# Float16 from the fourth set on: its preparation moved ahead, and its loads begun on ScalarE

## The chip, the cores and the metric

One core of a Trainium2 chip runs the whole program. The metric is the device time of one execution in microseconds; the kernel before took 2170.98 us, the median of three runs.

The engines have short names in the profile: PE (TensorE, the matmuls), PEld (its weight loads), DVE (VectorE), ACT (ScalarE), POOL (GpSimd) and SP (SyncE, which here only starts transfers). Each works through its own list of instructions in order.

## What is computed

A Fourier filter along the sequence, and then a sparse mixture of eight two-layer experts on its result, two of them per row:

```
y = irfft(rfft(x, axis=1) * (filt_r + 1j * filt_i))        # x: 8 x 2496 x 256
x = y.reshape(19968, 256)
noisy = x @ w_gate + log1p(exp(x @ w_noise)) * noise       # 8 experts
top2, top2_w = the two largest, and their softmax
for e in range(8):
    for k in range(2):
        mask = top2[:, k] == e
        h = maximum(x[mask] @ w1[e], 0)                    # 256 -> 1024
        out[mask] += top2_w[mask, k, None] * (h @ w2[e])   # 1024 -> 256
```

## The kernel before

**Sets and blocks.** The 8 batches are Fourier-transformed one after the other. After each one, `gate` and `route` choose experts and append the rows to lists of the experts in HBM. Whenever a batch is done, some blocks of 512 rows of one expert are certain to be full, and the program runs them while it transforms the next batch. I call the blocks that become possible with batch n set n. Blocks are numbered from 0: set 1 is blocks 0 and 1, set 2 is 2 to 11, set 3 is 12 to 17, set 4 is 18 to 23 (three pairs that share an expert's weights), set 5 is 24 to 33, and so on. At the end come shorter blocks.

**One block** (`expert`). POOL gathers 4 x 128 rows of y; they are transposed and split in two parts, xT. Layer 1 makes eight tiles `hps` of 128 x 512 in PSUM. Each product of two split numbers is three matmuls (`_mm3`, lines 124 to 126): high x high, high x low, low x high. For each tile ACT writes the high part of the relu, `hh` (L1371), and DVE the rest, the residual `hl` (L1372). Layer 2 makes four tiles `yps` of 128 x 256, which ACT scales by the gate (L1399) and POOL adds to the output in HBM (L1400). So a block has 48 matmuls in layer 1 and 96 in layer 2.

**Two forms of a split.** Up to set HALF - 1 = 4, high and low parts are fp32r, four bytes each. From set HALF = 5 on they are float16, which needs scales (powers of two) so that nothing leaves its range: one scale for y up to each batch (`xscale`), and two for each expert's weights (`wtab`).

**The scales of the weights** come from `wscales`, a generator of 88 or so steps that also loads, splits and stores all weights for the short blocks at the end. Its first part, up to the scales, must be done when the first float16 block is gathered. `run` takes one step of it for every READY / NPREP yields of `expert` (13 yields a block), with READY = 13 * 24 - 32 = 280 before. The steps are:

- 64 loads of a quarter of an expert's w1 or w2 into one of two buffers `wp` (`load`, L598, issued on SP), and two steps behind each the sum of its squares on ACT (`top`, L603). After every fourth, DVE takes the maximum over the four quarter sums (L605).
- two transforms of maxima into powers of two (`powers`, L555 to L577): a transpose on PE, about ten small operations on DVE, two matmuls `xm` on PE that spread the result over all partitions, and a copy to `wtab` (L648 to L652).
- 12 loads of y of the first two batches (L615, on SP, into the same buffers) and their maxima on DVE (`top_y`, L620). Later batches are reduced while y is still on the chip (L546).

POOL copies the scales of a slot's expert out of `wtab` (L1149), and with them the weights are split (L1203, L1204).

**What sets the order.** The program is written as one stream. A scheduler then places each instruction by its own model of time, within the dependencies. `pin` adds order among some instructions of an engine, and `self.after(i)` places an instruction behind i. The Fourier steps fill gaps between expert matmuls, so that PE's list mixes both.

## Time and profile before

| | us |
|---|---|
| median of three runs (2166.45, 2170.98, 2173.87) | 2170.98 |
| the profiled execution | 2166.25 |
| its span, first to last instruction | 2164.4 |
| PE busy in the span | 2096.1 (97%) |
| PEld | 1595.0 (74%) |
| DVE | 1468.0 (68%) |
| ACT | 1286.9 (59%) |
| POOL | 1023.6 (47%) |

Busy time is the union of an engine's instructions; PE's overlap, so a busy PE is not PE at its peak. What a change is worth is read from the stage that it touches, and there from the wait that ends last.

### The profile page before, as it was taken

What the parts mean: (1) busy time and instruction counts of PE and PEld (TensorE: products, weight loads), DVE (VectorE), ACT (ScalarE), POOL (GpSimd) and SP (SyncE); (2) the same over time, 40 slices, a digit from 0 to 9 for tenths busy, and PEclk for the clock granted to TensorE, in tenths of its full rate; (3) what the DMA queues carried; (4) which work ended last, traced back from release to release, by engine and by line L of the source; (5) the groups of instructions that cost most, each with busy time, mean ns of one, the idle gap of its engine ahead of it and who ended that gap; (6) DMA issues with size and microseconds to landing.
All of it is one profiled execution on the core that took longest, in us unless ns stands there. A gap on an engine that the chain in (4) does not pass through costs nothing.

```text
span 2164.4 us, 42794 instructions
## 1 busy us (share of the span) xinstructions
PE 2096.1 (97%) x14517; PEld 1595.0 (74%) x14517; DVE 1468.0 (68%) x3221; ACT 1286.9 (59%) x2505; POOL 1023.6 (47%) x946
## 2 busy tenths in 40 slices
PE   8779999999999999999999999999999999999997
PEld 6447888888888888666766677666666666667886
DVE  4866779787977896688665976589666664433443
ACT  6666875787676455756664565555566564333443
POOL 4223434443443334445444453555655565654554
PEclk9989999999999999999999999999999999999999
DMA  9688989998999766767766787666889999779997
GB/s 255 181 253 223 234 211 225 239 243 219 231 218 219 158 149 143 178 143 188 155 151 130 151 182 165 145 123 132 235 207 240 239 250 235 166 145 228 268 276 189
DMA packets 511673, 428.48 MB, mean 198 GB/s; under 512 B 215679, under 2 KB 397015, under 8 KB 511447
## 3 DMA queue, kind: packets, MB, share of 16 engines
q1 hardware_dynamic: 450135, 341.27, 59.2%
q0 software_dynamic: 61312, 84.40, 23.0%
q8 instruction: 116, 1.90, 0.4%
q14 instruction: 110, 0.90, 0.1%
HBM read 263.92 MB, written 122.03 MB: 178 GB/s over the span
## 4 chain that ended last, share of the span: by engine, by line
PE 84%; DVE 4%; DMA 3%; issue 3%; ACT 3%; SPq 1%; POOL 1%; POOLq 0%; ACTq 0%; DVEq 0%
PE yps L126 12%; PE yps L124 12%; PE yps L125 12%; PE hps L124 12%; PE hps L125 11%; PE hps L126 11%; PE q L448 3%; PE q L509 1%; PE u L461 1%; PE q L337 1%; DMA wp<-y 1%; ACT yt L541 1%; DVE hl L1372 1%; PE q L533 1%; DMA stage<-w 1%
## 5 line engine op out<-in xcount | busy, mean ns | idle before, releaser
L1372 DVE SCALAR_TENSOR_TENSOR hl<-hps,hh 128x512 f16<-128x512 f32 (+3 forms) x712 | 432.8, 624 | 357.4 <-ACT hh L1371 276.7
L1400 POOL DMA_INDIRECT out<-stage,ids x316 | 530.6, 1679 | 264.4 <-ACT stage L1399 171.9
L1158 POOL DMA_INDIRECT stage<-y,ids x316 | 348.7, 1103 | 541.8 <-DMA xt<-stage 441.0
L124 PE MATMUL yps<-w,hh 128*128 128x256 f16 (+1 forms) x2048 | 556.7, 278 | 5.1 <-ACT hh L1371 2.4
L125 PE MATMUL yps<-w,hh 128*128 128x256 f16 (+1 forms) x2048 | 551.2, 277 | 0.0
L126 PE MATMUL yps<-w,hl 128*128 128x256 f16 (+1 forms) x2048 | 541.5, 277 | 1.9 <-DVE hl L1372 1.8
L1371 ACT ACTIVATE hh<-hps 128x512 f16<-128x512 f32 (+3 forms) x712 | 376.2, 550 | 197.0 <-PE hps L126 172.9
L125 PE MATMUL hps<-mxl,w1h 128*128 128x512 f16 (+1 forms) x1024 | 394.3, 386 | 2.2 <-DVE mxl L1246 1.3
L126 PE MATMUL hps<-mxh,w1l 128*128 128x512 f16 (+1 forms) x1024 | 393.9, 385 | 0.0
L124 PE MATMUL hps<-mxh,w1h 128*128 128x512 f16 (+1 forms) x1024 | 385.7, 388 | 7.5 <-DVE hl L1372 6.7
L1399 ACT ACTIVATE stage<-yps,gt 128x256 f32<-128x256 f32 x316 | 143.2, 476 | 346.8 <-PE yps L126 192.0
L124 PEld LDWEIGHTS <-hh 128*128 128x128 f16 x1760 | 172.2, 98 | 54.4 <-issue 6.4
L126 PEld LDWEIGHTS <-hl 128*128 128x128 f16 x1760 | 171.4, 98 | 48.6 <-DVE hl L1372 2.4
L125 PEld LDWEIGHTS <-hh 128*128 128x128 f16 x1760 | 172.3, 98 | 34.3 <-issue 2.6
L124 PEld LDWEIGHTS yps<-w,hh 128*128 128x128 f32 x768 | 145.6, 190 | 11.4 <-ACT hh L1371 1.6
L126 PEld LDWEIGHTS yps<-w,hl 128*128 128x128 f32 x768 | 144.7, 190 | 10.5 <-DVE hl L1372 2.0
L125 PEld LDWEIGHTS yps<-w,hh 128*128 128x128 f32 x768 | 145.0, 190 | 4.5
L126 PEld LDWEIGHTS <-w1l 128*128 128x128 f16 x640 | 62.6, 98 | 71.7 <-issue 1.5
L541 ACT COPY yt<-q 117x1024 uint16<-117x1024 uint16 x96 | 90.7, 945 | 39.0 <-PE q L535 29.1
L1228 DVE COPY stage<-xt 128x1024 uint16<-128x1024 uint16 (+2 forms) x174 | 110.6, 689 | 1.4 <-issue 1.4
L1108 POOL CAST ids<-lt 128x4 int32<-128x4 f32 (+3 forms) x66 | 22.3, 338 | 171.8 <-DMA lt<-lst 171.6
L125 PEld LDWEIGHTS <-w1h 128*128 128x128 f16 x640 | 62.6, 98 | 52.9 <-issue 4.8
(286 smaller groups left out, 4067.0 us busy)
## 6 DMA issues: line engine op xcount, KB each, us to landing
stage<-w SPq DMA_DIRECT2D x328, 256.0 KB
x<-x SPq DMA_DIRECT2D x88, 256.0 KB
fd<-c SPq DMA_DIRECT2D x77, 240.0 KB
fi<-wpl SPq DMA_DIRECT2D x18, 1024.0 KB
fx<-fd SPq DMA_DIRECT2D x140, 128.0 KB
out<-z SPq DMA_DIRECT2D x24, 702.0 KB
wp<-w SPq DMA_DIRECT2D x64, 256.0 KB
fr<-w SPq DMA_DIRECT2D x16, 1024.0 KB
```

Of the source, the lines that this page charges most:

```text
L124: nc.tensor.matmul(o, lh, rh, start=start, stop=False)
L125: nc.tensor.matmul(o, lh, rl, start=False, stop=False)
L126: nc.tensor.matmul(o, ll, rh, start=False, stop=stop)
L448: nc.tensor.matmul(q3[:, :, 2 * j:2 * j + 2].rearrange("p b r -> p r b"), a[:, j], self.cV, start=True, stop=True)
L541: e = nc.scalar.copy(yt.bitcast(U16)[:, :k, :256].rearrange("p g (two d) -> p g two d", two=2), p.bitcast(U16)[:RP, :2 * m].rearrange("p ( ...
L1108: nc.gpsimd.tensor_copy(ids, t)
L1158: self.pin(lambda: nc.gpsimd.indirect_dma_start(out=x.bitcast(I32), out_offset=None, in_=self.y[:BLK + ready * ROWS], in_offset=bass.Indir ...
L1228: nc.vector.tensor_copy(xu.rearrange("p (t two) -> p two t", two=2), ent[3][0][:, 2 * kc:2 * kc + 2, :w])
L1371: self.relu = hold(lambda: nc.scalar.activation(h, p, AF.Relu))
L1372: v = hold(lambda: nc.vector.scalar_tensor_tensor(l, p, 0.0, hf[0], op0=ALU.max, op1=ALU.subtract))
L1399: nc.scalar.activation(o, p, AF.Copy, scale=gate[:, t])
L1400: a = nc.gpsimd.indirect_dma_start(out=self.io["out"][:BLK + ready * ROWS], out_offset=bass.IndirectOffsetOnAxis(ap=ids[:, t:t + 1], axis= ...
```

## The change

HALF goes from 5 to 4, so that set 4 (blocks 18 to 23) is computed in float16. READY becomes 13 * 18 - 62 = 172, so that the steps of the preparation come 1.95 yields apart instead of 3.2. The loads of weights for the sums of squares are issued by ACT instead of SP, behind the latest relu instead of behind SP's latest weight load. The loads and maxima of y move between the first 32 and the last 32 of these loads, ahead of the transforms. Their maxima on DVE, and those over the quarter sums, are placed behind the latest residual (`self.resid`); the latter also come two steps later and from two alternating buffers.

```diff
-HALF = 5
+HALF = 4
-READY = 13 * SETS[HALF - 2] - 32
+READY = 13 * SETS[HALF - 2] - 62
...
+        self.xst = cp.tile([128, NB, 2], F32, name="xst")
-        self.wquart = cp.tile([128, 4], F32, name="wquart")
+        self.wquart = cp.tile([128, 2, 4], F32, name="wquart")
...
-        t = self.xs[bt + 1] = self.cp.tile([128, 2], F32, name=f"xs{bt}")
+        t = self.xs[bt + 1] = self.xst[:, bt]
...
             t = self.P.tile([128, 512], F32, name="wp", bufs=2)
-            with self.after(self.spw):
-                nc.sync.dma_start(t, io["w1" if i < 4 * E else "w2"][i // 4 % E, i % 4])
+            with self.after(self.relu):
+                nc.scalar.dma_start(t, io["w1" if i < 4 * E else "w2"][i // 4 % E, i % 4])
             return t
 
         def top(i, t):
+            if i % 4 == 1 and i > 4:
+                quarts(i // 4 - 1)
             with self.after(self.relu):
-                nc.scalar.activation(t, t, AF.Square, accum_out=self.wquart[:, i % 4:i % 4 + 1])
-            if i % 4 == 3:
-                v.tensor_reduce(self.wmax[:, i // 4:i // 4 + 1], self.wquart, axis=AX.X, op=ALU.max)
+                nc.scalar.activation(t, t, AF.Square, accum_out=self.wquart[:, i // 4 % 2, i % 4:i % 4 + 1])
+
+        def quarts(a):
+            with self.after(self.resid):
+                v.tensor_reduce(self.wmax[:, a:a + 1], self.wquart[:, a % 2], axis=AX.X, op=ALU.max)
...
-            v.tensor_reduce(self.ymax[:RP, 2 * bt + h, g // 8:g // 8 + 1], t, axis=AX.X, op=ALU.max, apply_absolute_value=True)
+            with self.after(self.resid):
+                v.tensor_reduce(self.ymax[:RP, 2 * bt + h, g // 8:g // 8 + 1], t, axis=AX.X, op=ALU.max, apply_absolute_value=True)
...
-        yield from pairs(load, top, 8 * E)
+        yield from pairs(load, top, 0, 32)
+        yield from pairs(load_y, top_y, 0, len(Y))
+        self.known = True
+        while self.owed:
+            yield from self.xscale(self.owed.pop(0))
+        yield from pairs(load, top, 32, 8 * E)
+        quarts(2 * E - 1)
         for a, t in enumerate((TW1, TW2)):
...
-        yield from pairs(load_y, top_y, len(Y))
-        self.known = True
-        while self.owed:
-            yield from self.xscale(self.owed.pop(0))
...
+                self.resid = v
```

The scheduler moves more than the diff tells. The line numbers of the changed kernel are 1 to 9 higher from there on (L1371 becomes L1379, L1372 becomes L1380).

PE, before, at the end of block 16: its last second-layer matmuls (`yps`), three Fourier matmuls, and first-layer matmuls (`hps`) of block 17, of which 18 stand further ahead already.

```order
L125 MATMUL yps<-w_9333,hh 128x256
L126 MATMUL yps<-w_9333,hl 128x256
L345 MATMUL q_7661<-xh,hl 120x512
L346 MATMUL q_7661<-xh,hl 120x512
L347 MATMUL q_7661<-xl,hl 120x512
L124 MATMUL hps<-mxh_9468,w1h 128x512
L125 MATMUL hps<-mxl_9469,w1h 128x512
L126 MATMUL hps<-mxh_9468,w1l 128x512
```

PE, changed, at the end of block 17: its last second-layer matmul, then the first weight transform (L559 to L576) among Fourier steps.

```order
L126 MATMUL yps<-w_9805,hl 128x256
L559 MATMUL xm<-ident,wmax 8x128
L510 MATMUL q_7732<-ident,G 120x128 x4
L576 MATMUL xm<-pd,small 128x8
L449 MATMUL q_7757<-cf,a 128x2x64 x4
L346 MATMUL q_7780<-xh,hl 120x512
L347 MATMUL q_7780<-xh,hl 120x512
L348 MATMUL q_7780<-xl,hl 120x512
L576 MATMUL xm<-pd,small 128x8
L559 MATMUL xm<-ident,wmax 8x128
```

Eight rows further on, the list ends with the second transform's last matmul and the first float16 matmul of block 18.

```order
L576 MATMUL xm<-pd,small 128x8
L449 MATMUL q_8048<-cf,a 128x2x64 x4
L346 MATMUL q_8074<-xh,hl 120x512
L347 MATMUL q_8074<-xh,hl 120x512
L348 MATMUL q_8074<-xl,hl 120x512
L124 LDWEIGHTS w1h
L124 MATMUL hps<-mxh_9915,w1h 128x512
```

Before, the two transforms stood in blocks 21 to 23, and matmuls of a block's second layer and of the next block's first mixed; now no expert matmul stands between the end of block 17 and the second transform's end.

DVE, before, at the end of block 17: maxima over re-read y (L620) ahead of and between residuals (L1372).

```order
L620 TENSOR_REDUCE ymax<-wp 117x1
L546 TENSOR_REDUCE ymax<-yt 117x1
L620 TENSOR_REDUCE ymax<-wp 117x1
L442 MEMSET G 128x80
L620 TENSOR_REDUCE ymax<-wp 117x1 x3
L1372 SCALAR_TENSOR_TENSOR hl<-hps,hh 128x512
L620 TENSOR_REDUCE ymax<-wp 117x1
L1372 SCALAR_TENSOR_TENSOR hl<-hps,hh 128x512
```

DVE, changed, in block 6: the same maxima (L626 now), each behind a residual (L1380 now), beside the gating of the third batch.

```order
L1380 SCALAR_TENSOR_TENSOR hl<-hps,hh 128x512
L626 TENSOR_REDUCE ymax<-wp 117x1
L961 TENSOR_REDUCE df<-rank_102 117x22
L943 CAST hb<-bi 128x8
L974 TENSOR_SCALAR row<-to,small 56x1
L1000 TENSOR_SCALAR ci<-ci 8x1
L1380 SCALAR_TENSOR_TENSOR hl<-hps,hh 128x512 x2
L626 TENSOR_REDUCE ymax<-wp 117x1
```

All twelve moved from blocks 16 to 20 into blocks 5 to 7.

ACT, changed, from the last relu (L1379) of block 1's first layer on: loads (L599) and squares (L606) among Fourier copies and the scaled output (L1408).

```order
L1379 ACTIVATE hh<-hps 128x512
L1253 CAST mxh_2701<-stage 128x512
L606 ACTIVATE wp,wquart<-wp 128x512
L427 COPY b<-q_2038 64x512
L428 COPY b<-q_2038 64x512
L599 DMA wp<-w 128x512
L606 ACTIVATE wp,wquart<-wp 128x512
L450 COPY G<-q_2049 128x64x8
L599 DMA wp<-w 128x512
L606 ACTIVATE wp,wquart<-wp 128x512
L1408 ACTIVATE stage<-yps,gt 128x256 x2
L599 DMA wp<-w 128x512
```

Before, the loads stood in SP's list. Each square is that of the load before last: between the first load of these rows and the last square stand a square, the Fourier copy `G` and another load.

## Rows read from the trace of the kernel before

**Rows 1.** The page's part 4: shares of the chain that ended last, by engine.

```profile
PE 84%; DVE 4%; DMA 3%; issue 3%; ACT 3%; SPq 1%; POOL 1%; POOLq 0%; ACTq 0%; DVEq 0%
```

**Rows 2.** By stage: us; busy (count) PE,PEld,DVE,ACT,POOL; PE clock; DMA share; GB/s.

```profile
150.00:300.00 150.00, 145.71 (x919) 123.19 (x918) 103.62 (x219) 109.48 (x223) 54.07 (x47) 1.00 0.88 222
300.00:400.00 100.00, 97.77 (x650) 86.36 (x649) 89.58 (x227) 65.40 (x139) 49.05 (x40) 1.00 0.96 233
400.00:600.00 200.00, 199.01 (x1299) 174.92 (x1298) 164.39 (x361) 148.99 (x311) 79.37 (x68) 1.00 0.95 229
600.00:750.00 150.00, 143.73 (x923) 127.01 (x922) 114.58 (x205) 99.39 (x195) 57.70 (x47) 0.99 0.86 198
```

**Rows 3.** Groups by line and form: busy, mean ns | idle before, cause.

```profile
L125 PE MATMUL yps<-w,hh 128*128 128x256 f16 x1280 | 337.7, 273 | 0.0
...
L125 PE MATMUL hps<-mxl,w1h 128*128 128x512 f16 x640 | 242.0, 379 | 0.8 <-DVE mxl L1204 0.8
...
L125 PE MATMUL yps<-w,hh 128*128 128x256 f32 x768 | 213.6, 283 | 0.0
...
L125 PE MATMUL hps<-mxl,w1h 128*128 128x512 f32 x384 | 152.3, 397 | 1.3 <-DVE mxl L1246 1.3
```

**Rows 4.** Timeline of PE: start, duration in us, instruction.

```profile
703.49 0.28 PE L125 MATMUL yps<-w,hh 128*128 128x256 f32 x1
703.61 0.28 PE L126 MATMUL yps<-w,hl 128*128 128x256 f32 x1
...
1760.18 0.27 PE L125 MATMUL yps<-w,hh 128*128 128x256 f16 x1
1760.29 0.27 PE L126 MATMUL yps<-w,hl 128*128 128x256 f16 x1
```

**Rows 5.** Waits, 600 to 800 us: total us, count, longest.

```profile
DVE ymax L620 <- DMA wp<-y: 20.0, 6, 5.5
```

**Rows 6.** Timeline, DVE and PE; in brackets, us waited and for what.

```profile
666.89 1.22 DVE L620 TENSOR_REDUCE ymax<-wp 117x1 f32<-117x1024 bf16 x1 [5.04 <-DMA wp<-y]
...
668.76 0.50 PE L411 MATMUL q<-th,hl 128*128 128x512 f32 x1 [2.20 <-DVE tl L520]
...
710.64 1.22 DVE L620 TENSOR_REDUCE ymax<-wp 117x1 f32<-117x1024 bf16 x1 [0.93 <-DMA wp<-y]
...
712.51 0.80 PE L124 MATMUL hps<-mxh,w1h 128*128 128x512 f32 x1 [4.07 <-DVE hl L1372]
```

**Rows 7.** Tile `wp`: shortest/median/longest ns, first to last start.

```profile
L598 SPq DMA_DIRECT2D wp<-w x64: 108/375/1918, 161.4 to 618.1; - x64
...
L620 DVE TENSOR_REDUCE ymax<-wp x12: 947/1209/1220, 666.9 to 757.4; 117x1 f32<-117x1024 bf16 x8, 117x1 f32<-117x768 bf16 x4
```

**Rows 8.** Timeline, SP's queue and ACT: a load and its square.

```profile
567.29 0.52 SPq L598 DMA_DIRECT2D wp<-w  x1
...
570.33 0.63 ACT L603 ACTIVATE wp<-wp 128x512 f32<-128x512 f32 x1 [2.72 <-DMA wp<-w]
```

**Rows 9.** Waits, 150 to 640 us, of SP's queue and of ACT.

```profile
SPq L598 <- ACT wp L603: 30.7, 17, 5.6
...
ACT w1h L1322 <- DMA stage<-w: 18.5, 19, 3.5
```

**Rows 10.** Timeline from the first transform of the weights to block 24.

```profile
803.00 0.27 PE L558 MATMUL xm<-ident,wmax 128*8 128x128 f32 x1
...
806.38 0.14 DVE L562 TENSOR_SCALAR pe<-pm 8x1 int32<-8x1 int32 x1
...
810.88 0.68 DVE L546 TENSOR_REDUCE ymax<-yt 117x1 f32<-117x512 bf16 x1
...
814.33 0.17 DVE L648 COPY wtab<-xm 128x8 f32<-128x8 f32 x1 [2.17 <-PE xm L575]
...
836.04 0.44 POOL L1149 COPY sc<-wtab 128x3 f32 x3 [8.21 <-DVE wtab L652]
...
868.13 0.82 PE L124 MATMUL hps<-mxh,w1h 128*128 128x512 f16 x3
```

More of the change, by code (lines that the diff above doesn't have):

```diff
@@ L232, in setup @@
         self.ymax = cp.tile([128, 2 * NB, 6], F32, name="ymax")
+        self.xst = cp.tile([128, NB, 2], F32, name="xst")
         self.xm = cp.tile([128, 1], F32, name="xm")
         self.wmax = cp.tile([128, 2 * E], F32, name="wmax")
-        self.wquart = cp.tile([128, 4], F32, name="wquart")
+        self.wquart = cp.tile([128, 2, 4], F32, name="wquart")
         self.wtab = cp.tile([128, 3, E], F32, name="wtab")
         nc.vector.memset(self.ymax, 0.0)
-        self.xs, self.scaled, self.known, self.owed, self.relu = {}, False, False, [], None
+        self.xs, self.scaled, self.known, self.owed, self.relu, self.resid = {}, False, False, [], None, None
         self.rank = [cp.tile([RP, n, E], F32, name=f"rank{n}") for n in (39, 38)]
@@ L634, in split, with pairs @@
                 nc.sync.dma_start(self.wpl[e, a].rearrange("q p f -> p q f"), o)
-        def pairs(first, then, n):
+        def pairs(first, then, a, n):
             old = []
-            for i in range(n + 2):
-                if i >= 2:
+            for i in range(a, n + 2):
+                if i >= a + 2:
                     self.pin(then, *old.pop(0), hold=False)
```

## Prediction

> **What bounds the kernel now.** I read the chain that ended last first: TensorE (PE) makes up 84% of it [rows 1]. So a PE instruction that gets shorter shortens the end, and other work costs time only where PE has to wait for it. The table by stage comes next: from 150 to 600 us PE is busy for 442.5 of 450 us, VectorE (DVE) is the fullest of the others, with 89.6 of 100 us from 300 to 400, and ScalarE (ACT) has 126 us free of 450 [rows 2]. The stage from 600 to 750 us has the lowest PE share of the four, 143.7 of 150, so a stall must stand there; the waits of that stage name it (part 2).
>
> **Part 1, float16 for the fourth set.** Blocks 18 to 23 (three pairs of 512 rows) leave the two-part fp32r form; the order shows float16 weight loads from the first row of block 18 on. A block has 48 first-layer matmuls (8 x 2 x 3) and 96 second-layer ones (4 x 8 x 3). By line L125, which hardly waits, a first-layer matmul shows 397 ns in fp32r and 379 in float16, a second-layer one 283 and 273 [rows 3]. These durations overlap, so I check them by starts: two second-layer matmuls start 0.12 us apart in fp32r and 0.11 in float16 [rows 4], the same 10 ns. A block saves 48 x 18 + 96 x 10 ns = 1.82 us, six save **10.9 us**. The starts of the second layer alone give 96 x 10 ns x 6 = 5.8 us, my lower end. The extra scaling of splits on DVE and ACT is hidden: at the start of block 18 DVE is at 76% [rows 2], and no DVE instruction is added per split.
>
> **Part 2, the stall that goes.** In the old place, the twelve maxima over re-read y stand between blocks 16 and 20. DVE waits 20.0 us for their loads, in six waits [rows 5]. PE feels it twice: it stands 2.20 us before L411, whose operand DVE writes behind one of these maxima, and 4.07 us within block 18's first layer, where the next bank `hps` comes free with a residual that stands among maxima on DVE [rows 6]. Both go: **6.3 us back**; the lower end is 4.1, if the first had another cause as well.
>
> **Part 3, the same maxima in the new place.** They now stand in blocks 5 to 7, each behind a residual of the first layer, around 335 to 378 us. Their work is 12 x 1.2 = 14.4 us [rows 7] and falls where DVE is 90% busy: such 43 us hold about 4.5 us of free DVE. The order shows what gives way: Fourier steps come up to a block later, relative to the expert blocks, until block 17. Deferred work is not lost, and between first layers no residual is due. I take **2 us** on PE; the ends are 0 and the old price, 6.3.
>
> **Part 4, loads issued on ACT.** ACT gets 64 issues. On SP one took 375 ns [rows 7]; at that price ACT has 24 us more to do, beside squares that now fall into some 400 us instead of 460. Behind each issue stand copies and relus, for which DVE and then PE wait. The costlier part is a wait: in 13 places, nearly all at the end of a first layer, a square stands one to three instructions behind its own load, with 0.8 to 2.7 us of ACT work between (an estimate from the durations of those instructions). Before, a load for which its square waited was used 3.04 us after its issue [rows 8]. So 13 times about 1.3 us: 17 us of ACT idling, most of it in a second layer, when PE asks ACT for little but Fourier copies, and against 126 us that were free [rows 2]. I take **1 us** on PE; the upper end is all 17 us, the lower end a gain of 2. That gain would come from SP: it stood 30.7 us before these loads for ACT's squares, with weight loads and gathered rows' transposes queued behind. But ACT's 18.5 us of waits for staged weights [rows 9] reach PE in no row that I found, so I count no gain. A rule speaks against one as well: the Trainium skill, DMA: Bandwidth & Descriptors, section Issuing engines are not separate DMA queues, says that issuing on several engines saves only the sequencer's time to start a transfer. By that rule the move is worth nothing on the transfers, and the sum stays; the trace adds that a wait ahead of the issue is saved too.
>
> **Part 5, a new wait at block 18.** The scales of the weights must exist before block 18's first matmul, not block 24's. Two transforms (maxima turned to powers of two, through PE and about ten small DVE operations each) end in the table, from which POOL copies the slot's scales, with which ACT and DVE split the weights. In the old order POOL's copies start at 836.04 us and block 24's float16 matmuls at 868.13 [rows 10]: 32 us of lead. In the new one both transforms stand between block 17's last matmul and block 18's first, with only Fourier steps beside them. The first took 11.5 us before (803.00 to 814.50), stretched by other work. From the order I count on DVE, from the first transform to the first split, 12 operations of full width at 0.68 us and 26 small ones at 0.14 [rows 10], 11.8 us; two round trips to PE add about 1, POOL's copies 0.5, ACT's first split about as much as a wide DVE operation, 0.7: 14 us. PE has beside it 12 matmuls of 512 columns (0.24 us each, twice the 256 of [rows 4]), 14 narrower ones of 0.11 or so, and the transforms' own 1 us: 5.5 us. PE idles **8.5 us**. The ends: 2, if no Fourier step stands in the chain's way (3.6 + 1 + 1.2 us for the chain alone, plus the 2 us of Fourier work that PE then does with nothing else beside it); 19, if both transforms take as long as the first did (23 + 1.2 - 5.5).
>
> **Sum.** -10.9 - 6.3 + 2 + 1 + 8.5 = **-5.7 us**. The profiled execution took 2166.25 us (span 2164.4), 4.7 below the median 2170.98 of three runs, which reach from 2166.45 to 2173.87. So 2160.5 for an execution like the profiled one, and **2165 us** beside the median. A measurement of this kernel tells about 0.3%, 6.5 us, from no change: the forecast lies just inside that bound.
>
> **The rivals.**
> - *A, the forecast,* 2158 to 2171: chance 0.42, of which 0.24 lies below the bound and 0.18 within it.
> - *B, block 18 costs little.* If PE's Fourier work covers the chain, part 5 costs 2 and parts 3 and 4 nothing: -15, 2156 us. For it: PE waited for no scale before. Against: the first weight load stands behind the whole chain. 0.14.
> - *C, block 18 takes it all back.* Part 5 costs 15, towards its upper end: +0.8, 2172 us. For it: the 11.5 us of one transform [rows 10]. Against: that one had expert work in between. 0.16 (0.13 within the bound, 0.02 faster, 0.01 slower).
> - *D, ACT's queue decides, slower.* A load on ACT and the square right behind it hold back a copy that PE's next matmul needs. It decides from the point where the landing takes longer than ACT's own work between, which the 13 places reach at 3.04 us. If each holds PE for its 1.3 us: -5.7 - 1 + 17 = +10.3, 2181 us, and more if the landings are later than that. For it: 0.95 of the DMA engines' time is taken from 400 to 600 us [rows 2]. Against: second layers ask little of ACT. 0.18 (0.16 beyond the bound, 0.02 within).
> - *E, DVE decides in blocks 5 to 7.* The 10 us that don't fit into 43 us reach PE as 8: +0.3, 2171 us. For it: 89.6% [rows 2]. Against: the order moves Fourier steps away. 0.10 (0.08 within, 0.01 on either side).
>
> That the change doesn't do what it says is out: the order shows float16 from block 18.
>
> **The numbers.** Faster: 0.24 + 0.14 + 0.02 + 0.01 = 0.41. Within: 0.18 + 0.13 + 0.02 + 0.08 = 0.41. Slower: 0.01 + 0.16 + 0.01 = 0.18. The range leaves out the further third of B and the further half of D: 2153 to 2182. A's own range is 2158 to 2171.
>
> **What would show it.** Part 1: by form, L125's fp32r matmuls are 288 instead of 384 in the first layer, 576 instead of 768 in the second. Part 2: no DVE wait for re-read y after 600 us. Part 3: the maxima between 330 and 380 us, DVE near 100% there. Part 4: among the waits, ACT's squares on their own loads with some 17 us, few PE waits on ACT. Part 5: between block 17's last second-layer matmul and the first float16 one some 14 us, 8 to 9 of them PE waiting for DVE and ACT. I am wrong if that stretch is under 8 or over 20 us, or if PE's waits for ACT between 150 and 560 us grow by more than 5 us.

## The result and the profile after

The changed kernel took 2186.52 us (median of six runs, 2180.97 to 2194.48), the kernel before, on the same chip, 2171.86 (six runs). The ratio is 1.0071, with a 95% interval of 1.0055 to 1.0086: **slower by 15 us**, where 6 us faster had been forecast. The time lies outside the stated range of 2153 to 2182. The profiled execution took 2183.05 us, with a span of 2181.3.

The table by stage of the changed kernel, columns as in [rows 2], with one stage more:

```profile
150.00:300.00 150.00, 146.38 (x904) 123.30 (x903) 102.03 (x218) 112.95 (x237) 51.54 (x46) 0.97 0.94 235
300.00:400.00 100.00, 92.38 (x591) 80.95 (x589) 91.97 (x208) 55.68 (x113) 43.12 (x33) 0.98 0.95 215
400.00:600.00 200.00, 195.13 (x1245) 171.54 (x1244) 148.16 (x323) 146.62 (x306) 87.42 (x71) 0.98 0.92 220
600.00:750.00 150.00, 139.56 (x873) 115.67 (x875) 114.37 (x244) 95.03 (x177) 53.64 (x47) 0.95 0.77 184
750.00:900.00 150.00, 146.14 (x1037) 101.32 (x1032) 117.02 (x278) 89.11 (x168) 71.18 (x63) 1.00 0.72 161
```

PE's busy time fell where it had been highest: from 97.8 to 92.4 of 100 us between 300 and 400, from 199.0 to 195.1 of 200 between 400 and 600. There the **granted clock** is 0.97 or 0.98, where [rows 2] have 1.00. ACT has less to do from 300 to 400 (55.7 instead of 65.4 us), while DVE is fuller (92.0). By tiles, ACT has 14 squares fewer there (16 instead of 30, as the loads of y take their steps) and 9 Fourier copies fewer (tiles `b`, `th` and `yt`); from 600 to 750 us it has 4 copies `b` and 2 `yt` more than before.

The same table in narrow windows shows the clock, here where it fell, and then the one such window between 160 and 740 us in which it fell in the kernel before:

```profile
200.00:220.00 20.00, 16.61 (x88) 14.55 (x87) 14.15 (x25) 13.99 (x30) 8.53 (x9) 0.84 1.10 281
380.00:400.00 20.00, 18.50 (x118) 15.70 (x118) 19.92 (x43) 8.27 (x18) 2.49 (x2) 0.91 0.89 202
460.00:480.00 20.00, 16.88 (x95) 15.16 (x94) 10.09 (x17) 12.72 (x30) 10.60 (x10) 0.83 1.01 238
700.00:720.00 20.00, 15.56 (x104) 14.00 (x102) 11.34 (x27) 10.69 (x19) 10.13 (x8) 0.89 0.86 201
720.00:740.00 20.00, 17.61 (x74) 11.38 (x74) 13.11 (x32) 13.43 (x23) 2.57 (x7) 0.77 0.49 138
```

```profile
700.00:720.00 20.00, 15.93 (x105) 13.34 (x105) 12.89 (x19) 9.43 (x22) 3.54 (x4) 0.91 0.81 178
```

A share of 0.84 over 20 us is 6.4 us at 1.2 instead of 2.4 GHz. Behind six of PE's pauses, of some 1.5 to 5 us, the clock is at the lower level for some 3 to 7 us. From 140 to 740 us that makes 36 us at 1.2 GHz, against 6 in the kernel before, and PE idles in 5 of the 36. So pauses cost twice: once as idle time, and once as (36 - 5 - 6) / 2 = 12.5 us of slower matmuls. The mean granted clock of all executions says the same: 0.983 to 0.987 in the six of the change, 0.991 on average in the 18 of the kernel before that ran beside e1 to e4. What is missing to full clock, times the span, is 32 us against some 20. So the clock is at most 13 of the 15 us. The timeline shows the second part behind a wait of 1.54 us; second-layer matmuls start 0.21 us apart instead of 0.12 [rows 4]:

```profile
214.78 0.58 PE L124 MATMUL yps<-w,hh 128*128 128x256 f32 x1 [1.54 <-ACT hh L1379]
...
216.23 0.41 PE L124 MATMUL yps<-w,hh 128*128 128x256 f32 x1
216.44 0.41 PE L125 MATMUL yps<-w,hh 128*128 128x256 f32 x1
```

Three of the pauses, in the timeline of the changed kernel. At 381 us a residual stands behind a maximum over y (L626), four parts of split weights (L1331) and the third batch's routing:

```profile
374.39 1.21 DVE L626 TENSOR_REDUCE ymax<-wp 117x1 f32<-117x1024 bf16 x1
375.52 2.48 DVE L1331 TENSOR_TENSOR w<-stage,w 128x512 fp32r<-128x512 f32 x4
...
380.15 0.69 DVE L1070 TENSOR_TENSOR oc<-half,lo 117x512 f16<-117x512 f16 x1
380.75 0.69 DVE L1380 SCALAR_TENSOR_TENSOR hl<-hps,hh 128x512 fp32r<-128x512 f32 x1
381.50 0.80 PE L124 MATMUL hps<-mxh,w1h 128*128 128x512 f32 x1 [4.74 <-DVE hl L1380]
```

At 467 us ACT waits 3.34 us for a square's own load, and the Fourier copies behind it come late, then DVE's product, then PE:

```profile
466.65 0.63 ACT L606 ACTIVATE wp<-wp 128x512 f32<-128x512 f32 x1 [3.34 <-DMA wp<-w]
...
469.93 0.69 DVE L431 TENSOR_TENSOR a<-a,b 128x512 f32<-128x512 f32 x1
...
470.67 1.01 PE L449 MATMUL q<-cf,a 128*128 128x128 f32 x3 [3.12 <-DVE a L431]
```

And between blocks 17 and 18, from PE's last fp32r matmul at 712.25 to its first float16 one at 731.82, stand both transforms:

```profile
712.25 0.28 PE L126 MATMUL yps<-w,hl 128*128 128x256 f32 x1
712.37 0.27 PE L559 MATMUL xm<-ident,wmax 128*8 128x128 f32 x1
712.68 0.28 DVE L561 TENSOR_REDUCE pm<-xm 8x1 f32<-8x128 f32 x1 [1.51 <-PE xm L559]
717.46 0.35 DVE L572 TENSOR_SCALAR pd<-ident,pq 8x8 f32<-8x8 f32 x2
717.73 0.59 PE L576 MATMUL xm<-pd,small 8*128 8x8 f32 x2 [4.38 <-DVE pd L572]
...
725.45 0.35 PE L576 MATMUL xm<-pd,small 8*128 8x8 f32 x2 [2.04 <-DVE pd L572]
...
728.67 0.43 POOL L1157 COPY sc<-wtab 128x3 f32 x3 [11.35 <-DVE wtab L664]
728.93 2.56 ACT L1211 ACTIVATE w1h<-stage,sc 128x512 f16<-128x512 f32 x4
...
731.82 0.65 PE L124 MATMUL hps<-mxh,w1h 128*128 128x512 f16 x1
```

**How I add up.** I call PE's *lag* in a stretch what its instructions take there, from each start to the next, beyond what the quicker quarter of the same form takes in the kernel before, added up from the timeline. It holds waits and slow clock alike. From 150 to 600 us it is 28.8 us before and 45.0 after, from 600 to 900 us 24.6 and 29.9, over the whole span 153.7 and 178.4. Of these 24.7 us float16 gives back 9.2 by the quick starts (48 x 14 and 96 x 9 ns, six times); 15.5 are left, and the spans differ by 16.9. A lag is that of one profiled execution; two executions of one kernel can differ by some us in it. The profiled execution of the kernel before is 6 us below the median of its six, e5's is 12 and e13's 8 below their own, e9's 7 above; the others lie within 5 us.

### The profile page after: what moved, and what is told of

It is laid out like the page before. It is cut to its first block, busy times and chain, and to the rows that moved or that the text cites. A ratio compares the mean times of both kernels' runs of the same rounds, so it can differ in the third digit from the quotient of the medians.

```text
span 2181.3 us, 42780 instructions
## 1 busy us (share of the span) xinstructions
PE 2096.7 (96%) x14522; PEld 1561.2 (72%) x14522; DVE 1472.6 (68%) x3231; ACT 1291.7 (59%) x2505; POOL 1028.1 (47%) x955
## 4 chain that ended last, share of the span: by engine, by line
PE 61%; DVE 4%; issue 1%; ACT 1%; DMA 1%; POOL 0%; SPq 0%; DVEq 0%; POOLq 0%; ACTq 0%
PE yps L126 9%; PE yps L124 9%; PE yps L125 9%; PE hps L125 9%; PE hps L124 9%; PE hps L126 9%; PE q L449 1%; DVE hl L1380 1%; PE q L510 1%; PE u L462 1%; PE q L534 0%; PE q L536 0%; PE q L535 0%; PE q L412 0%; PE q L414 0%
## 5 line engine op out<-in xcount | busy, mean ns | idle before, releaser
L1380 DVE SCALAR_TENSOR_TENSOR hl<-hps,hh 128x512 f16<-128x512 f32 (+3 forms) x712 | 433.7, 625 | 351.0 <-ACT hh L1379 260.9
L1166 POOL DMA_INDIRECT stage<-y,ids x316 | 340.3, 1077 | 532.5 <-DMA xt<-stage 439.5
L1379 ACT ACTIVATE hh<-hps 128x512 f16<-128x512 f32 (+3 forms) x712 | 377.0, 550 | 198.8 <-PE hps L126 171.8
L124 PE MATMUL hps<-mxh,w1h 128*128 128x512 f16 (+1 forms) x1024 | 384.3, 387 | 10.9 <-DVE hl L1380 10.9
L1408 ACT ACTIVATE stage<-yps,gt 128x256 f32<-128x256 f32 x316 | 143.4, 475 | 340.8 <-PE yps L126 161.9
L124 PEld LDWEIGHTS <-hh 128*128 128x128 f16 x1952 | 190.9, 98 | 58.8 <-issue 8.3
L126 PEld LDWEIGHTS <-hl 128*128 128x128 f16 x1952 | 190.1, 98 | 54.4 <-DVE hl L1380 2.5
L125 PEld LDWEIGHTS <-hh 128*128 128x128 f16 x1952 | 191.0, 98 | 37.0 <-issue 2.0
L126 PEld LDWEIGHTS <-w1l 128*128 128x128 f16 x736 | 72.0, 98 | 84.7 <-issue 4.2
L124 PEld LDWEIGHTS yps<-w,hh 128*128 128x128 f32 x576 | 110.7, 193 | 11.3 <-ACT hh L1379 5.2
L126 PEld LDWEIGHTS yps<-w,hl 128*128 128x128 f32 x576 | 110.3, 193 | 10.8 <-DVE hl L1380 3.6
L125 PEld LDWEIGHTS <-w1h 128*128 128x128 f16 x736 | 72.1, 98 | 61.5 <-issue 6.1
L124 PEld LDWEIGHTS <-w1h 128*128 128x128 f16 x736 | 72.0, 98 | 59.2 <-issue 6.9
L125 PEld LDWEIGHTS yps<-w,hh 128*128 128x128 f32 x576 | 110.3, 193 | 3.9 <-DVE w L1331 1.0
```

The source lines that it names most:

```text
L124: nc.tensor.matmul(o, lh, rh, start=start, stop=False)
L125: nc.tensor.matmul(o, lh, rl, start=False, stop=False)
L126: nc.tensor.matmul(o, ll, rh, start=False, stop=stop)
L1166: self.pin(lambda: nc.gpsimd.indirect_dma_start(out=x.bitcast(I32), out_offset=None, in_=self.y[:BLK + ready * ROWS], in_offset=bass.Indir ...
L1379: self.relu = hold(lambda: nc.scalar.activation(h, p, AF.Relu))
L1380: v = hold(lambda: nc.vector.scalar_tensor_tensor(l, p, 0.0, hf[0], op0=ALU.max, op1=ALU.subtract))
```

## The experiments

All ratios are to the kernel before, on the same chip; 0.1% is 2.2 us. The difference of two ratios has an interval of some 5 us either way (6 where one has six runs), so that differences of 4 to 9 us are barely clear of the noise or not at all. "Ahead" is the number of Fourier matmuls (the tiles `q`) in the trace that stand ahead of the end of block 17's first layer; what is done in a gap at block 18 comes on top. The expectations have such numbers from the order, ahead of block 18; they are 286 to 310 lower, and the trace doesn't show them. "Gap" is the time from the last fp32r second-layer matmul to the first float16 first-layer one in the profiled execution, at block 18 with HALF = 4 and at block 24 with HALF = 5; a negative gap means that the first float16 block's first layer already stands among the second layer ahead of it.

| kernel | HALF, READY | maxima over y, blocks | ahead | gap, us | lag 150-600, 600-900 | ratio and interval |
|---|---|---|---|---|---|---|
| before | 5, 280 | 17 to 20 | 1109 | -14.4 | 28.8, 24.6 | 1 |
| the change | 4, 172 | 5.8 to 7.1 | 1035 | 19.6 | 45.0, 29.9 | 1.0071 (1.0055-1.0086) |
| e1 own bank | 4, 172 | 5.8 to 7.1 | 1016 | -12.7 | 43.4, 31.3 | 1.0046 (1.0030-1.0061) |
| e2 loads on SP | 4, 172 | 5.8 to 7.1 | 1035 | 17.9 | 47.3, 26.5 | 1.0031 (1.0013-1.0048) |
| e3 y late | 4, 172 | 10.4 to 12 | 1054 | 21.7 | 46.6, 35.4 | 1.0079 (1.0055-1.0103) |
| e4 | 5, 172 | 5.8 to 7.1 | 1048 | 20.1 | 46.2, 27.3 | 1.0051 (1.0035-1.0066) |
| e5 before's code | 4, 172 | 10 to 12.4 | 1031 | 21.6 | 49.0, 24.3 | 1.0087 (1.0065-1.0110) |
| e6 | 5, 280 | 9 to 11.9 | 1101 | -14.8 | 38.7, 9.0 | 0.9948 (0.9929-0.9966) |
| e7 own bank | 4, 222 | 7 to 9.2 | 1129 | -10.0 | 45.7, 11.2 | 0.9956 (0.9941-0.9971) |
| e8 before's code | 5, 270 | 16 to 18.4 | 1129 | -10.7 | 37.3, 18.8 | 0.9982 (0.9964-1.0000) |
| e9 own bank, y late | 4, 172 | 10.4 to 12 | 1101 | -17.0 | 56.7, 9.3 | 0.9955 (0.9937-0.9973) |
| e10 no maxima over y | 4, 172 | none | 1082 | -16.4 | 36.1, 10.9 | 0.9906 (0.9885-0.9926) |
| e11 own bank | 5, 222 | 7 to 9.2 | 1137 | -8.9 | 45.3, 9.7 | 0.9985 (0.9969-1.0001) |
| e12 own bank, SP | 4, 222 | 7 to 9.2 | 1126 | -16.0 | 48.5, 15.7 | 0.9980 (0.9961-0.9998) |
| e13 own bank | 4, 192 | 6.1 to 8 | 1126 | -17.0 | 46.2, 15.3 | 1.0003 (0.9987-1.0019) |
| e14 | 4, 210 | 7 to 9 | 1069 | 55.6 | 47.8, 52.6 | 1.0153 (1.0125-1.0181) |
| e15 own bank | 4, 236 | 7.8 to 10 | 1137 | -11.6 | 35.5, 15.4 | 0.9926 (0.9900-0.9953) |
| e16 own bank, y late | 4, 192 | 11.8 to 13.5 | 1115 | 0.1 | 45.7, 14.6 | 0.9973 (0.9954-0.9991) |

### First round: the parts of the change, undone one by one

**e1, a bank of their own for the transforms.** `powers` takes its PSUM tile from the three banks `fps` that all Fourier steps share, in program order; so a transform can't pass a Fourier step that was written ahead of it. Here it gets another bank:

```diff
-        q = self.ps("xm")
+        ring = (lambda: self.PS.tile([128, 512], F32, name="xm", tag="xps", bufs=1)) if squared else (lambda: self.ps("xm"))
+        q = ring()
...
-        a, e, s = P.tile([E, 1], F32, name="pm")[:n], P.tile([E, 1], I32, name="pe")[:n], P.tile([E, 2], I32, name="pq")[:n]
+        if squared:
+            o = P.tile([E, 4], I32, name="wo")[:n]
+            a, e, s = o[:, 0:1].bitcast(F32), o[:, 1:2], o[:, 2:4]
+        else:
+            a, e, s = P.tile([E, 1], F32, name="pm")[:n], P.tile([E, 1], I32, name="pe")[:n], P.tile([E, 2], I32, name="pq")[:n]
...
-        d = P.tile([E, 2, E], F32, name="pd")[:n, :, :n]
+        d = P.tile([E, 2, E], F32, name="wd" if squared else "pd")[:n, :, :n]
...
-        q = self.ps("xm")[:, :2 * n].rearrange("p (j n) -> p j n", j=2)
+        q = ring()[:, :2 * n].rearrange("p (j n) -> p j n", j=2)
```

> The changed kernel, but the weights' transforms take their PSUM bank from the third bank of the first layers (tag xps) and their small tiles from buffers of their own, so that they no longer queue behind the Fourier steps: they stand in blocks 12.6 to 13.1 instead of between blocks 17 and 18. Theory (the gap at block 18 is the largest single loss): the 19.5 us from block 17's last second-layer matmul to block 18's first matmul fall to the 5 to 6 us that Fourier steps take there, and the time falls by 10 to 14 us against the change, to about +3 us against the kernel before (2175). Rival (block 18 waits for the scale of y as well, which the order shows at 18.0 in this kernel): a chain of the same kind stays, the gap is still over 10 us, and the time falls by less than 6 us, to +9 or more.

Measured: 1.0046, some 5 us below the change. The gap is gone altogether (float16 matmuls begin 12.7 us ahead of the last fp32r one), yet only half of what I expected came back. The lag from 600 to 900 us is as large as in the change: it has moved into other waits. So with the maxima where they are the gap is not the largest loss. The rival's reason, the scale of y, shows in no wait at block 18, but it does at block 24, where the next set starts. Block 24's first matmul comes 7.6 us behind block 23's last there (in the change it comes 16.7 us ahead of it), and the longest of PE's waits between 600 and 900 us stands in between, of a Fourier step for DVE's copy of that scale (`xst`):

```profile
883.85 0.27 PE L126 MATMUL yps<-w,hl 128*128 128x256 f16 x1
...
889.16 0.78 PE L346 MATMUL q<-xh,hl 117*120 117x512 f32 x1 [3.64 <-DVE xst L593]
...
891.45 1.02 PE L124 MATMUL hps<-mxh,w1h 128*128 128x512 f16 x2
```

**e2, the loads on SP again.**

```diff
-            with self.after(self.relu):
-                nc.scalar.dma_start(t, io["w1" if i < 4 * E else "w2"][i // 4 % E, i % 4])
+            with self.after(self.spw):
+                nc.sync.dma_start(t, io["w1" if i < 4 * E else "w2"][i // 4 % E, i % 4])
```

> The changed kernel with the 64 loads of weights for the sums issued on SP again, behind its latest weight load. Theory (ACT's queue costs a part only): the stall at 470 us (PE 3.1 us, and 6.8 us at half clock) goes, the one at 212 us may go, and the time falls by 4 to 8 us, to +7 to +11 us against the kernel before. Rival (ACT's queue is the whole loss, as my case D had it): the time falls by 12 us or more, to within 3 us of the kernel before. Second rival (all of it is elsewhere): no change, +15.

Measured: 1.0031, 9 us below the change (some 5 either way), about as the theory had it. The reason is another one, though. ACT's wait for the loads of its squares, from 150 to 640 us, is in the change

```profile
ACT wp L606 <- DMA wp<-w: 25.3, 12, 4.1
```

and with the loads on SP

```profile
ACT wp L606 <- DMA wp<-w: 44.9, 14, 5.5
```

The wait that I had blamed grew by 20 us, and the kernel got faster. What the 9 us come from is not settled by this pair.

**e3, maxima over y behind all 64 loads of weights.**

```diff
-        yield from pairs(load, top, 0, 32)
+        yield from pairs(load, top, 0, 8 * E)
         yield from pairs(load_y, top_y, 0, len(Y))
...
-        yield from pairs(load, top, 32, 8 * E)
         quarts(2 * E - 1)
```

> The changed kernel with the loads and maxima of re-read y behind all 64 loads of weights instead of between the first 32 and the last 32: the maxima stand in blocks 10.4 to 12 instead of 5.8 to 7.1. Theory (maxima over y among the third batch's gating cost PE waits for residuals of 2.0 and 4.7 us and 3.4 us at half clock): those waits go, and the time falls by 5 to 9 us, to +6 to +10 us against the kernel before. Rival (they cost as much wherever a residual stands behind them): PE waits of the same size in blocks 10 to 12 and no change, +15.

Measured: 1.0079, no gain, as the rival said. Even without maxima there, PE stands 4.00 us at 386 us, behind ACT's relu. The gap at block 18 is 21.7 us, with the clock at 1.2 GHz for 17 us.

**e4, the preparation of the change without float16 in set 4.**

```diff
-HALF = 4
+HALF = 5
-READY = 13 * SETS[HALF - 2] - 62
+READY = 13 * SETS[2] - 62
```

> The changed kernel with float16 from the fifth set again (HALF = 5; READY stays 172): the preparation of the change without its use. The transforms stand in blocks 18.4 to 19.4, amid expert matmuls, and nothing waits for them until block 24. Theory (preparation costs some 16 us between 150 and 600 us, block 18's wait 14, float16 gives 11): without the wait and without the gain the time is 3 us below the change, about +12 us against the kernel before. Rival (the loss is all at block 18, and the preparation is cheap): the time is at or below that of the kernel before. Second rival (float16 in set 4 gives nothing): 14 us below the change, +1.

Measured: 1.0051, 4 us below the change, as the theory had it, though within the noise. The preparation costs 11 us by itself. The loss isn't block 18's alone: here the weights' transforms end at 737 us, and yet a gap of 20.1 us stands ahead of block 24, with late Fourier steps, the transform of the scale of y and then block 24's own splits in it:

```profile
877.26 0.28 PE L126 MATMUL yps<-w,hl 128*128 128x256 f32 x1
...
897.36 1.01 PE L124 MATMUL hps<-mxh,w1h 128*128 128x512 f16 x2 [4.58 <-ACT mxh L1211]
```

### Second round: the pace

**e5, the kernel before with HALF = 4 and READY = 172.**

```diff
-HALF = 5
+HALF = 4
-READY = 13 * SETS[HALF - 2] - 32
+READY = 13 * SETS[HALF - 2] - 62
```

> The kernel before with HALF = 4 and READY = 172 and nothing else of the change: loads on SP, maxima over y behind all of them, no order behind residuals. In it the transforms stand in blocks 17.4 to 18, the maxima over y in blocks 10 to 12. Theory (the pace of the preparation, one step in 1.95 yields instead of 3.2, is what costs some 17 us between 150 and 600 us in all kernels so far): about as slow as the change, +10 to +18 us against the kernel before, with PE 15 us or more behind its nominal pace beyond that of the kernel before in that stretch. Rival (the other edits cost it: loads on ACT, the new place and order of the maxima): the stretch costs under 6 us, and the time is between -5 and +5.

Measured: 1.0087. With the transforms on the Fourier steps' banks, the pace and float16 are enough for the loss; none of the change's other edits is needed for it. That it isn't the pace by itself is shown by e9.

**e6, the change's edits at the old pace, set 4 in fp32r.**

```diff
-HALF = 4
+HALF = 5
-READY = 13 * SETS[HALF - 2] - 62
+READY = 13 * SETS[HALF - 2] - 32
```

> The changed kernel with HALF = 5 and READY = 280 as before: the edits of the change (loads on ACT, maxima over y in the middle, maxima behind residuals) at the old pace and without float16 in set 4. Theory (the pace costs it): PE's lag between 150 and 600 us is within 5 us of that of the kernel before, and the time within 4 us of it. Rival (the edits cost it): +8 us or more, with the lag of 15 us in that stretch.

Measured: 0.9948, faster than theory and rival had it: the edits gain 11 us. The lag from 150 to 600 us is 10 us larger than before, where the theory allowed 5. Against e4, which differs in READY alone, it is 22 us. The stages in question, first of e4 and then of e6:

```profile
600.00:750.00 150.00, 147.70 (x953) 130.81 (x953) 116.58 (x241) 98.86 (x187) 64.39 (x49) 1.00 0.81 192
750.00:900.00 150.00, 140.79 (x923) 122.32 (x922) 108.47 (x267) 80.92 (x153) 54.32 (x47) 0.95 0.61 144
```

```profile
600.00:750.00 150.00, 150.00 (x975) 132.91 (x974) 112.34 (x229) 112.66 (x233) 61.11 (x50) 1.00 0.95 224
750.00:900.00 150.00, 149.52 (x980) 127.90 (x979) 116.86 (x279) 92.69 (x173) 66.38 (x58) 1.00 0.70 163
```

Both have done their maxima over y by 600 us and both transform behind it, yet the slow pace keeps PE busy for 299.5 of 300 us and the fast pace for 288.5. One thing that differs is how many Fourier steps are already done: 1101 matmuls ahead of the end of block 17's first layer, against 1048.

**e7, own bank and READY = 222.** The diff of e1, and

```diff
-READY = 13 * SETS[HALF - 2] - 62
+READY = 13 * SETS[HALF - 2] - 12
```

> The changed kernel with the transforms on a bank and buffers of their own, as in the first experiment, and READY = 222 in place of 172: they now stand in blocks 16 to 16.5, and the steps come 2.5 yields apart. Theory (pace): the lag between 150 and 600 us falls by about half, 8 us, and with block 18's wait gone the time is 0 to 5 us below that of the kernel before. Rival (the pace does not matter): as the first experiment, +8 to +10.

Measured: 0.9956, 20 us below e1, which differs in READY alone, and 10 below the kernel before, where the theory had 5 at most. Most of it lies where the theory had not put it: the lag from 150 to 600 us is no smaller, the one from 600 to 900 falls from 31.3 to 11.2.

**e8, a control: the kernel before with another READY.**

```diff
-READY = 13 * SETS[HALF - 2] - 32
+READY = 13 * SETS[HALF - 2] - 42
```

> The kernel before with READY = 270 instead of 280 and nothing else: the same work, its order shifted a little. A control of how much the order alone moves the time. Theory (losses have mechanisms, and an order near the old one costs what the old one costs): within 3 us of the kernel before. Rival (the old order is a lucky one among orders that are all alike, and any other loses 8 us or more): +6 or more.

Measured: 0.9982, 4 us faster, with an interval of 0 to 8. The old order is no lucky one.

### Third round: what the pace does

**e9, own bank and y late together, READY = 172** (the diffs of e1 and e3).

> The changed kernel at READY = 172 with the first experiment's own bank and buffers for the transforms, and with the maxima over y behind all 64 loads, in blocks 10.4 to 12. By the order, 803 Fourier matmuls then stand ahead of block 18, against 730 in the first experiment at the same pace, 745 in the change and 807 in the kernel before. Theory (the maxima over y, put into blocks 5.8 to 7.1 at this pace, push the Fourier steps back, and what is pushed back is made up ahead of block 18, where nothing covers its waits; the pace by itself costs little): -3 to -10 us against the kernel before, as READY = 222 gave, and PE's lag between 600 and 900 us is under 15 us against 31 in the first experiment. Rival (the pace by itself costs it, through loads, squares and transfers): as the first experiment, +8 to +12.

Measured: 0.9955, the theory. The pace is that of e1 and of the change. Beside an own bank the place of the maxima makes 20 us (and with it the last 32 loads, which start at 323 us here and at 378 in e1); on the Fourier steps' banks it makes nothing (e3). Neither edit does it alone (1.0046 and 1.0079), both do: 25 us below the change. The stages of e1 and of e9:

```profile
600.00:750.00 150.00, 140.95 (x914) 116.31 (x913) 112.81 (x229) 95.84 (x177) 59.90 (x53) 0.99 0.79 185
750.00:900.00 150.00, 141.35 (x996) 96.63 (x994) 117.71 (x280) 89.21 (x167) 63.26 (x58) 0.99 0.67 150
```

```profile
600.00:750.00 150.00, 150.00 (x988) 127.95 (x986) 114.53 (x228) 106.62 (x203) 63.13 (x54) 1.00 0.86 199
750.00:900.00 150.00, 148.73 (x1039) 103.94 (x1037) 123.51 (x285) 95.98 (x176) 76.08 (x64) 1.00 0.78 171
```

ACT shows it best: from 600 to 750 us it does 106.6 us of work beside a full PE, against 95.8 beside a PE that idles for 9. ACT still waits 23.2 us for its loads in e9, so these waits are not what PE feels.

**e10, no maxima over y at all.**

```diff
-        Y = [(bt, h, g) for bt in range(FIRSTS) for h in range(2) for g in range(0, NG, 8)]
+        Y = []
```

> The changed kernel without the 12 loads of y and their maxima (the scales of y then know nothing of the first two batches; the rest is the change's, READY = 172, transforms on the Fourier steps' banks). By the order 788 Fourier matmuls stand ahead of block 18 and the transforms in blocks 16.4 to 16.8, by themselves. Theory (the maxima over y push Fourier steps and transforms back): no gap at block 18, and -5 to -14 us against the kernel before. Rival (the pace): +5 or more.

Measured: 0.9906, 36 us below the change, more than the theory's range. At the change's pace, with its loads on ACT and its transforms on the Fourier steps' banks, leaving out the maxima takes away the whole loss and more. Two things go at once, though: the work, and twelve steps of the generator, so that the last loads and the transforms come 12 x 1.95 yields, 1.8 blocks, earlier by that alone. So the run doesn't show that the maxima are what had pushed the transforms to block 18.

**e11, e7 with HALF = 5.**

```diff
-HALF = 4
+HALF = 5
-READY = 13 * SETS[HALF - 2] - 12
+READY = 13 * SETS[2] - 12
```

> The kernel of the seventh experiment (own bank, READY = 222) with HALF = 5: the same preparation at the same pace, set 4 in fp32r. It gives what float16 in set 4 is worth by itself. Theory (10.9 us, by the starts of the matmuls): 8 to 13 us slower than the seventh experiment, so -2 to +3 us against the kernel before. Rival (given back, as the splits of float16 take DVE and ACT longer or block 18 waits for its scales anyhow): within 4 us of the seventh experiment.

Measured: 0.9985, that is 6.3 us slower than e7, with some 5 us either way by the two intervals, so between theory and rival. Float16 in set 4 gains; the interval holds my lower end of 5.8 as well as the 10.9 of the sum.

**e12, e7 with the loads on SP** (the diff of e2).

> The kernel of the seventh experiment (own bank, READY = 222) with the 64 loads on SP again. Theory (at this pace few squares stand right behind their own load, and where the load is issued matters little): within 4 us of the seventh experiment, -5 to -13 us against the kernel before. Rival (the loads on ACT are what gains at a slow pace): 6 us or more slower than the seventh.

Measured: 0.9980, 5 us slower than e7, with some 5 us either way, so between theory and rival. At this pace the loads on ACT are no loss, and perhaps a gain, while at READY = 172 they cost 9 us (e2).

### Fourth round: the two causes apart, and a better version

**e13, e1 with READY = 192.** The diff of e1, and

```diff
-READY = 13 * SETS[HALF - 2] - 62
+READY = 13 * SETS[HALF - 2] - 42
```

> The first experiment (own bank for the transforms, maxima over y in the middle) with READY = 192 instead of 172. The maxima over y stand in blocks 6.1 to 8, as close to the third batch's gating as before, but 820 Fourier matmuls stand ahead of block 18 instead of 730. Theory (what is pushed back is what costs): -4 to -10 us against the kernel before, as READY = 222, and PE's lag between 600 and 900 us under 15 us. Rival (the maxima among gating and residuals cost it where they stand): +4 us or more.

Measured: 1.0003, between the two. The lag from 600 to 900 us is 15.3, just above what the theory allowed, with 1126 matmuls ahead; but from 300 to 400 us it is 17.1, where the kernel before has 5.8. That could be maxima that cost where they stand, but e9 has 12.8 there without them. The count of Fourier steps is not the whole story.

**e14, the change with READY = 210.**

```diff
-READY = 13 * SETS[HALF - 2] - 62
+READY = 13 * SETS[HALF - 2] - 24
```

> The changed kernel with READY = 210 and nothing else: the maxima over y in blocks 7 to 9, 775 Fourier matmuls ahead of block 18, the transforms still between blocks 17 and 18. Theory (two separate losses: the pushed-back Fourier steps, half restored here, and the gap at block 18 of some 8 to 14 us, which stays): 0 to +8 us against the kernel before. Rival (the gap costs little, as the 5 us of the first experiment suggest): -4 us or less.

Measured: 1.0153, twice the loss of the change, at a slower pace; neither had it. The gap has grown to 55.6 us, because the fifth batch's gating and routing now stand in it too. Its PE timeline, waits only, and one of its windows:

```profile
748.01 0.53 PE L935 MATMUL rk<-rs,small 117*117 117x8 f32 x2 [11.06 <-DVE rs L919]
757.27 0.37 PE L1073 MATMUL ra<-oc 117*128 117x56 f16 x4 [8.18 <-DVE oc L1069]
765.32 0.59 PE L576 MATMUL xm<-pd,small 8*128 8x8 f32 x2 [5.60 <-DVE pd L572]
```

```profile
740.00:760.00 20.00, 3.53 (x26) 2.65 (x26) 18.89 (x84) 1.64 (x3) 0.00 (x0) 0.50 0.06 17
```

These matmuls take their banks from the same ring as the transforms, in program order. Block 18 waits for the transforms, and so for all that is ahead of them in the ring. What stands in the gap is a matter of order, and it isn't small: e7, with own bank and READY 222, is 43 us faster.

**e15, e1 with READY = 236.** The diff of e1, and

```diff
-READY = 13 * SETS[HALF - 2] - 62
+READY = 13 * SETS[HALF - 2] - -2
```

> The seventh experiment with READY = 236 instead of 222, as slow as block 18 allows (the last steps come with its gather). The maxima over y stand in blocks 7.8 to 10, 827 Fourier matmuls ahead of block 18. Theory: -8 to -14 us against the kernel before. Rival (the last steps, taken at once at block 16, cost what the pace gains): -4 us or more.

Measured: 0.9926 (0.9900 to 0.9953), 16 us below the kernel before: a version that is faster than both kernels and computes all of it.

**e16, e9 with READY = 192** (the diffs of e1, e3 and e13).

> The ninth experiment (own bank, maxima over y behind all loads) with READY = 192: the maxima in blocks 11.8 to 13.5, 813 Fourier matmuls ahead of block 18. Theory: as the ninth or a little better, -8 to -14 us against the kernel before. Rival (the maxima late push back the steps that block 18 waits for, the order shows the scale of y at 18.0): 0 or slower.

Measured: 0.9973, inside neither range. Maxima that come later still, in blocks 11.8 to 13.5, do no better; the gap is 0, not -17. Against e13, which has this pace too and the maxima in the middle, it is 6.5 us, some 5 either way: what the place is worth falls with the pace.

## Why the prediction was wrong

The step that failed is parts 3 and 5 of the sum, the maxima in their new place and the gap at block 18: taken as two separate losses of 2 and 8.5 us, 10.5 in all. With both undone (e9) the kernel is 25 us faster than the change, with one undone 5 us (e1) or not at all (e3). The sum was off by 21 us; 14.5 of them are these two terms. The other parts together had -16.2 us, and e9 has -10. Neither sign that the prediction named for being wrong came up: the stretch at block 18 is 19.6 us, and PE's waits for ACT fell.

**Part 1, float16: right in kind.** The counts by form are as said, and so are the durations:

```profile
L125 PE MATMUL yps<-w,hh 128*128 128x256 f16 x1472 | 388.1, 273 | 0.0
L125 PE MATMUL hps<-mxl,w1h 128*128 128x512 f16 x736 | 278.3, 379 | 2.3 <-DVE mxl L1212 2.3
L125 PE MATMUL yps<-w,hh 128*128 128x256 f32 x576 | 162.0, 286 | 0.4 <-DVE w L1331 0.4
L125 PE MATMUL hps<-mxl,w1h 128*128 128x512 f32 x288 | 114.7, 399 | 0.1
```

By itself it measured 6.3 us (e11 against e7) where the sum had 10.9; the interval holds both. By the quick starts a first-layer matmul gains 14 ns, not the 18 of the durations, and a second-layer one 9: with them the sum would have had 9.2.

**Part 2, the old stall: right.** DVE waits no more for re-read y after 600 us, and at the old pace the lag from 600 to 900 us falls from 24.6 to 9.0 (e6). There parts 2 to 4 together measured -11 us where the sum has -3.3: at the old pace the same edits gain.

**Part 3, the maxima in the new place: priced at nothing where it counted.** The prediction took 2 us, with 6.3 as the upper end, because "deferred work is not lost, and between first layers no residual is due". Moving them is worth 20 us beside an own bank (e9 against e1) and nothing without one (e3). The place was forecast:

```profile
L626 DVE TENSOR_REDUCE ymax<-wp x12: 932/1196/1242, 334.9 to 381.4; 117x1 f32<-117x1024 bf16 x8, 117x1 f32<-117x768 bf16 x4
```

and so was DVE's load there (19.92 of 20 us from 380 on). What I read in the order and then priced at nothing was the Fourier steps that come up to a block later. A batch's Fourier steps and gating must be through before the set that builds on it starts. The traces show the push: the fifth batch's gating, needed by block 24, starts 34 us later in the change than before, 45 later in e1, and 11 later in e9. Its first matmul, before and in the change:

```profile
749.71 0.28 PE L927 MATMUL rk<-rs,small 117*117 117x8 f32 x2
```

```profile
783.68 0.28 PE L935 MATMUL rk<-rs,small 117*117 117x8 f32 x2
```

What is pushed back is done at the start of a set, where few expert matmuls are left to fill PE while a Fourier step goes from PE to ACT to DVE and back: in the change ahead of block 18, with 77 Fourier matmuls between block 17's last first-layer matmul and block 18's first (9 before), in e1 and e4 ahead of block 24. In all runs "ahead" and the lag behind 600 us go together, in two groups: up to 1069 matmuls the lag is 24 us or more, from 1082 on under 20, but for the kernel before with its own stall. That the push causes the lag is argued from this; what the runs show by undoing it is that the place of the maxima, the pace and the bank decide together.

**Part 4, loads on ACT: the size is in the range, the mechanism is not shown.** ACT waited 25.3 us in 12 waits for its squares' loads (17 in 13 were forecast). PE's waits for ACT between 150 and 560 us did not grow (3.5 us before, 2.2 after); its waits for DVE did, from 2.9 to 13.4, and behind some of these stands a late copy of ACT, as in the rows at 467 us, so that the sign I had named could not show it. At this pace the loads on ACT cost 9 us (e2), at a slower one they cost nothing (e12), some 5 us either way. The rule that I cited, the Trainium skill, DMA: Bandwidth & Descriptors, section Issuing engines are not separate DMA queues, says that issuing on several engines saves only the sequencer's time to start a transfer. Here one such move cost 9 us in one order and nothing in another; whether that comes from the 64 issues on ACT (335 ns each) or from what stood behind their waits, no run shows.

**Part 5, the gap at block 18: right in place, short in size.** 19.6 us against 14 forecast, at the upper end. PE's waits in it are 4.38 and 2.04 us. For the other 13 PE works, on what takes about 6 by the quick starts: from 715 to 732 us the clock was at 1.2 GHz but for 3 us. I saw that the transforms stood there, but not why: that they share a ring of banks with Fourier steps. Taking them off the ring gains 5 us with the maxima in the middle (e1), where the pushed-back steps then come due at block 24, and 27 with the maxima late (e9 against e3).

**What the sum left out** is the clock altogether, 12.5 us by the rows. In the same stretch, from 140 to 740 us, PE of the kernel before idles for 16 us instead of 29, and its clock falls once instead of six times (a fall just ahead of 140 us stands in both). It goes with the pauses: e9's mean granted clock over its nine executions is 0.991, as in the kernel before. What is missing to full clock, times the span, is 20 us there against 32 in the change, so the clock is at most 12 of the 25 us between the two.

**The rivals.** D (ACT's queue, 0.18) came nearest in time, at 2181 us, but its price of 17 us for ACT's queue measured 9 (e2), and with the loads on ACT still in place e9 has no loss. E named the right place and the right engine and priced it at 8 us, where it measured 20 beside an own bank and nothing without. The forecast's form, a sum of terms each with the rest of the order held still, is what misled: e1, e3 and e9 show that two of the terms don't add up.

## What to carry to other kernels

When a change moves work into a stage whose engines are full, don't price it by that stage alone: list what the scheduler pushes out, find the next point that needs it, and price it there without cover. A small step that draws its buffer from another stream's ring stands in that stream's order; give it a buffer of its own before anything is made to wait for it. And where PE is busy to the last per cent, a pause of a few microseconds is to be priced with the slower clock that follows it.

## What the runs showed that I had not expected

- The clock can fall behind pauses of only 1.5 to 5 us, and is at 1.2 GHz for some 3 to 7 us then; behind pauses of 2.2 us in the kernel before it did not. In e14 it stayed there for 41 us in one piece.
- A slower pace can make the loss larger (e14: 33 us at READY = 210, 15 at 172), when it only changes what else stands ahead of the transforms.
- A wait can grow by 20 us while the kernel gets 9 us faster (e2).
- Open: what the loads on SP gain at READY = 172; and how the 25 us of parts 3 and 5 divide into Fourier steps pushed back, residuals held up in place, and the clock.
